# A planned attention-plus-MLP kernel: separate due times for the early work, first chunks first, and own places for minima and last sums

## The chip, the cores and the metric

The kernel runs on one core of a Trainium2 chip. The metric is the device time of one execution in microseconds (us). A core has five engines that run side by side, each in its own program order: TensorE (PE) for matmuls, VectorE (DVE), ScalarE (ACT) and GpSimd (POOL) for elementwise work, and SyncE (SP), which here issues all transfers between the main memory (HBM) and the on-chip memory (SBUF). Matmuls write into eight accumulation banks (PSUM). An engine waits only where an instruction needs something that another engine or a transfer has not finished.

## The reference

Inputs are `q`, `k`, `v` of 4 sequences x 8 heads x 768 positions x 64, and two weight matrices, `w_in` (512 x 2048) and `w_out` (2048 x 512). What is computed, cut to its core:

```python
keep = (pos_k < n_global) | ((rel >= 0) & (rel < n_local))     # 8 global keys, 96 local ones
scores = q @ k.T / sqrt(64) - slope[head] * dist               # then -1e9 where not keep
a = exp(scores - max(scores)); a = a / (sum(a) + 1e-9)
x = heads of (a @ v) side by side                              # 3072 tokens x 512
h = x @ w_in
out = (h * cos(h)) @ w_out                                     # 3072 x 512
```

## The kernel before

**Tiling.** The 3072 tokens are eight chunks of 384: two for each of the four sequences. The second chunk of a sequence needs 96 keys of the chunk ahead of it, the first does not, so of its four 96-row blocks the first has a window of 96 columns where all others have 200. For each chunk there are four pairs of heads (`plan_unit`, `plan_values`), 32 pairs in all: load keys and queries, scores on PE, a fold of the two halves of the window (L559) and a subtract-and-minimum (L568) on DVE, `exp` on ACT (L593), reciprocal (L604), normalisation (L616 where the block is the short one, else L621) on DVE or POOL, transposes on PE (L683), two masked copies (L691, L696) on DVE, the product with `v` on PE (L718), and a split of the result into a rounded high part and a rest (`xh` L735, `xl` L739). The first eight pairs ("exact") multiply in one pass (L542); later ones split keys and queries into two parts (`plan_split`) and use L546.

The MLP runs in 128 steps, each a chunk with one 128-wide block of the hidden layer (`plan_step`): 12 matmuls against `w_in` (L754, "first product"), an argument reduction (ACT L771, DVE L774), the cosine (ACT L777), a product (DVE L814), a split into `gh` and `gl` (L823, L827), and 9 matmuls against `w_out` (L765, "second product"). The sums over the blocks stay in PSUM until `plan_store` copies them out. `plan_weights` loads the 64-bit weight words (512 KB a block and matrix) and joins them into high part and rest, with work for ACT, DVE and POOL (L392 to L424).

**What sets the order.** Every operation goes into a planner (`Plan`) with the engines that may run it, a rough cost on each, the places it needs, and possibly a due time. `dues` carries due times backwards: an operation's due is the smaller of its own and what those that need it leave it. `run` then plays the program through with those costs: a free engine takes the ready operation with the earliest due, and one that several engines may run goes to the one where wait plus cost times `WEIGHT` is least. The outcome is a fixed program order for each engine. `PHASES` gives the order of steps: the first six blocks for chunk 0, then sixteen for chunk 1, then the remaining ten for chunk 0, then chunk by chunk. `DEPTH` is how far ahead of the transfers SP may run in the play.

**Fills.** `emit` puts matmuls of zeros (L1068, "fills") on PE where its plan shows a gap in the first 100 us: ten at the head, and one for every 250 ns of a gap beyond 150 ns (500 ns in the first 7 us). A fill thus marks a planned gap.

**Due times before.** `xdue` gives the four pairs of chunk 0 dues 5000 apart and those of chunk 1 6000 apart (`EARLY`); later chunks follow `MARGIN` and `EACH`. A step's due is its number times `PERIOD`; weights have no due of their own.

**The rest touched.** `worst` (L584) is one 128 x 8 tile: after a pair's minima are in its `st` tile, DVE folds them into `worst`. At the end `flag` reduces `worst` to a word (L873), every engine reads it (L1010) and branches over a general path that does not run (L1011). The output copies `oo` (L849) of all chunks use the two places `wu`, shared with the weights' scratch; the third copy of a chunk so needs the first one's store to have finished.

Of the kernel before, what the change touches and what calls it, by code (L numbers as in the profile page):

```python
# [10 lines left out]
F32 = mybir.dt.float32  # L11
# [34 lines left out]
MARGIN, EACH = 3.2, 3.2  # L46
EARLY = {0: 5000, 1: 6000}
WEIGHT = {PE: 1, ACT: 0.5, DVE: 1.2, POOL: 0.6}

PHASES = [(0, 0, 6), (1, 0, 16), (0, 6, 16)]  # L50

PIECES = {-1: [(0, 128), (128, 384)]}
NT, NST, NPV, NX, NV, NRAW, NQK, NRR, NG = 5, 5, 3, 2, 3, 3, 2, 3, 2

DEPTH = 3000

# [191 lines left out]
class Net:  # L248
# [26 lines left out]
    def constants(self):  # L275
# [47 lines left out]
        g.memset(self.half_pi, math.pi / 2)  # L323
        self.worst = self.const.tile([P, 2 * CT], F32, name="worst")
        g.memset(self.worst, -3.0e38)
# [46 lines left out]
    def plan_weights(self, f):  # L372
# [5 lines left out]
        ends = []  # L378
        for kind, src, out in (("wi", cols, self.wi), ("wo", rows, self.wo)):
            raw = self.const.tile([P, 512, 2], U32, name="raw", tag=f"{kind}{f}")  # L380
# [51 lines left out]
            o = p.op({ACT: 525, DVE: 335, POOL: 595}, whigh, [o], [wu], port=True)  # L432
            ends.append(p.op({DVE: 600, POOL: 1260}, wrest, [o], [wu], port=True))
        return ends


    def plan_loads(self, n, b2):


        nc, p, D = self.nc, self.plan, self.D  # L440
        b, c = divmod(n, self.NCH)
        W = 2 * UB * D
        t0 = c * CW
        lead = 1 if c == 0 else 0
        vs = Slot(self.early("v", n, b2), lambda i: self.work.tile([SLOT, 1 + CT, W], F32, name="v", tag=i))
        L = dict(n=n, first=c == 0, v=vs)
        src = self.v[b][:, b2 * W : (b2 + 1) * W]
        nt = 1 + CT - lead
        s = t0 - (1 - lead) * R

        def blocks(e):
            nc.sync.dma_start(vs.tile[:R, lead:], src[s : s + nt * R].rearrange("(t p) d -> p t d", p=R))

        def glob(e):
            nc.sync.dma_start(
                vs.tile[R:, lead:CT], src[:G].rearrange("p (t d) -> p t d", t=1).broadcast_to([G, CT - lead, W])
            )

        L["lv"] = [
            p.op({SP: 470}, blocks, [], [vs], extra=290 * nt),  # L460
            p.op({SP: 470}, glob, [], [vs], extra=46 * CT),
        ]
        return L
# [18 lines left out]
    def plan_unit(self, L, pr):  # L482
# [6 lines left out]
        n, first = u["n"], u["first"]  # L489
        b, c = divmod(n, self.NCH)  # L490
        u["hs"] = slice((pr % UB) * P, (pr % UB + 1) * P)
# [25 lines left out]

        st = u["st"] = Slot("st", lambda i: self.work.tile([R, 6 * CT], F32, name="st", tag=i))
        tt = u["tt"] = [
# [8 lines left out]
        for js, h in [(js, h) for js in (((0, 1),) if exact else ((0,), (1,))) for h in range(0, CT, 2)]:  # L528
# [25 lines left out]
            for j, ps in pss.items():  # L554
# [7 lines left out]
                for i, t in enumerate(ts):  # L562

                    def least(e, i=i, t=t, j=j, ps=ps):
# [10 lines left out]
                            scalar=3.0e38,  # L575
                            accum_out=st.tile[:, at : at + 1],
                        )
# [3 lines left out]
        n2 = 2 * CT  # L581

        def worst(e):
            nc.vector.tensor_tensor(self.worst[:R], self.worst[:R], st.tile[:, :n2], op=ALU.max)  # L584

        self.chain("worst", p.op({DVE: 100}, worst, [o for _, o in ttr], [st], due=self.xdue(n, pr), port=True))
        exps = []
        for (t, j), o in ttr:

            def exp(e, t=t, j=j):  # L590
                x = tt[t // 2].tile[:, t % 2, j, : width(t)]
                c = 2 * t + j
                nc.scalar.activation(  # L593
                    x, x, AF.Exp, bias=st.tile[:, c : c + 1], scale=-1.0, accum_out=st.tile[:, n2 + c : n2 + c + 1]
                )

            exps.append(p.op({ACT: 365}, exp, [o], [tt[t // 2], st], table="exp"))

        def add(e):
            x = st.tile[:, n2 : 2 * n2]  # L600
            nc.vector.tensor_scalar(x, x, 1e-9, None, op0=ALU.add)

        def rec(e):
            nc.vector.reciprocal(st.tile[:, 2 * n2 :], st.tile[:, n2 : 2 * n2])  # L604

# [3 lines left out]
        for h in range(0, CT, 2):  # L609

            def norm(e, h=h):
                x = tt[h // 2].tile.rearrange("p t j w -> p (t j) w")
                r = st.tile[:, 2 * n2 + 2 * h : 2 * n2 + 2 * h + 4].rearrange("p (c o) -> p c o", o=1)
                if lead(h):
# [129 lines left out]
    def xdue(self, n, pr):  # L744
        rest = self.NP - 1 - pr
        first = next(s for s, x in enumerate(self.seq) if x[0] == n)
        if n in EARLY:
            return first * PERIOD - rest * EARLY[n]
        return int((first - MARGIN - rest * EACH) * PERIOD)
# [29 lines left out]
    def plan_step(self, s, n, f, a, b):  # L779

        nc, p = self.nc, self.plan
        due = s * PERIOD
        x = self.x[n]
# [57 lines left out]
    def plan_store(self, n, t, po, o, keep, due):  # L841
# [5 lines left out]
        else:  # L847
            oo = Slot("wu", lambda i: self.work.tile([P, 512], F32, name="oo", tag=i))
        if before is not None and keep:  # L849
# [11 lines left out]
        if keep:  # L861
            return
        r0 = n * CW + t * P
        p.op({SP: 470}, lambda e: nc.sync.dma_start(self.out[r0 : r0 + P, :], oo.tile), [o], [oo], extra=730)


    def flag(self):
# [4 lines left out]
        fi = self.small.bitcast(I32)[0:1, 15:16]  # L872
        nc.vector.tensor_reduce(c[:, 0:1], w, axis=mybir.AxisListType.X, op=ALU.max)  # L873
        nc.vector.tensor_scalar(c[:, 0:1], c[:, 0:1], -FILL - 1024.0, None, op0=ALU.is_le)
# [262 lines left out]
```

## Time and profile before

| what | value |
|---|---|
| time, median of 3 | 696.05 us (695.97 to 697.09) |
| the profiled execution's own time | 695.79 us |
| its span, first to last instruction | 694.1 us |
| PE busy | 680.9 us (98%) |
| DVE busy | 485.3 us (70%) |
| ACT busy | 459.2 us (66%) |
| POOL busy | 172.0 us (25%) |
| fills | 55, 16.1 us of PE's busy time |

The span is what the trace covers; the time around it is 1.7 us. Busy time of PE includes the fills, which compute nothing, so PE is to be read stage by stage: in which stretch it does matmuls of the computation, and in which it fills or waits. An idle engine costs nothing unless something that sets the end waits for it.

### The profile page before, as it was taken

How to read it: one execution, taken by the hardware profiler on the slowest of the kernel's cores; microseconds unless marked ns; L12 is line 12 of the kernel's file. 1: busy time of each engine (PE TensorE's matmuls, PEld its weight loads, DVE VectorE, ACT ScalarE, POOL GpSimd, SP SyncE). 2: the span in 40 equal slices, each digit the busy share in tenths (PEclk: the TensorE clock that was granted, in tenths of full speed). 3: DMA queues.
4: the chain of work that ended last, by engine and by line, in shares of the span. 5: the costliest groups of instructions: out<-in, count | busy, mean ns of one | idle time of the engine just before them, and what ended most of it. 6: DMA issues, size and time to landing. Idle time of an engine off the chain costs nothing.

```text
span 694.1 us, 12978 instructions
## 1 busy us (share of the span) xinstructions
PE 680.9 (98%) x4473; PEld 594.3 (86%) x4473; DVE 485.3 (70%) x1477; ACT 459.2 (66%) x1144; POOL 172.0 (25%) x221
## 2 busy tenths in 40 slices
PE   7999999999999999999999999999999999999995
PEld 4667899889898988989889888888889888898994
DVE  7998888987648877577757777477773787534342
ACT  7899986889746675576646666476663766544442
POOL 5666645553202121111111112011120111200000
PEclk9999999999999999999999999999999999999999
DMA  8999601215204222032321321132230300001001
GB/s 283 304 344 285 174 1 48 59 47 139 64 1 114 64 60 60 1 106 65 69 69 38 105 65 48 44 102 60 53 95 0 115 27 1 1 1 46 0 1 51
DMA packets 32603, 55.74 MB, mean 80 GB/s; under 512 B 3472, under 2 KB 18192, under 8 KB 32528
## 3 DMA queue, kind: packets, MB, share of 16 engines
q1 hardware_dynamic: 32528, 54.82, 27.5%
q8 instruction: 37, 0.61, 0.4%
q14 instruction: 38, 0.31, 0.2%
HBM read 48.52 MB, written 6.29 MB: 79 GB/s over the span
## 4 chain that ended last, share of the span: by engine, by line
PE 84%; ACT 5%; DVE 4%; DMA 4%; POOL 1%; issue 1%; SPq 0%; ACTq 0%; POOLq 0%; DVEq 0%
PE bank L765 36%; PE bank L754 36%; PE bank L546 5%; PE bank L718 5%; PE bank L683 2%; DMA raw<-in_qk_dram 2%; DMA raw<-in_w_out_dram 1%; ACT tt L593 1%; DVE tt L568 1%; POOL tt L616 1%; ACT L593 1%; ACT L777 1%; DVE bank L559 1%; ACT rr L777 0%; ACT raw L408 0%
## 5 line engine op out<-in xcount | busy, mean ns | idle before, releaser
L754 PE MATMUL bank<-xh,w 128*128 128x384 f32 x1024 | 296.9, 342 | 0.0
L765 PE MATMUL bank<-w,gh 128*128 128x512 f32 x768 | 245.5, 401 | 0.0
L754 PEld LDWEIGHTS bank<-xh,w 128*128 128x128 f32 x1024 | 188.2, 188 | 8.3 <-DVE rr L814 0.6
L754 PE MATMUL bank<-xl,w 128*128 128x384 f32 x512 | 172.9, 338 | 0.2 <-DVE xl L739 0.2
L765 PEld LDWEIGHTS bank<-w,gh 128*128 128x128 f32 x768 | 137.8, 188 | 20.1 <-issue 0.3
L765 PE MATMUL bank<-w,gl 128*128 128x512 f32 x384 | 151.5, 394 | 0.0
L774 DVE SCALAR_TENSOR_TENSOR rr<-rr,bank 128x384 f32<-128x384 int32 x129 | 70.1, 544 | 105.1 <-ACT rr L771 104.9
L771 ACT ACTIVATE rr<-bank 128x384 int32<-128x384 f32 x129 | 62.3, 483 | 119.8 <-PE bank L754 115.8
L777 ACT ACTIVATE rr<-rr,half_pi 128x384 f32<-128x384 f32 x129 | 79.0, 614 | 38.3 <-DVE rr L774 37.4
L814 DVE TENSOR_TENSOR rr<-bank,rr 128x384 f32<-128x384 f32 (+1 forms) x121 | 66.6, 551 | 48.4 <-ACT rr L777 47.9
L754 PEld LDWEIGHTS bank<-xl,w 128*128 128x128 f32 x512 | 96.4, 188 | 4.3 <-DVE xl L739 0.4
L593 ACT ACTIVATE tt<-tt,st 96x104 f32<-96x104 f32 (+1 forms) x256 | 94.3, 370 | 4.8 <-DVE st L568 4.2
L765 PEld LDWEIGHTS bank<-w,gl 128*128 128x128 f32 x384 | 72.1, 188 | 17.3
L827 DVE TENSOR_TENSOR gl<-rr,gh 128x384 fp32r<-128x384 f32 x102 | 60.4, 592 | 13.2 <-ACT gh L268 5.7
L268 ACT CAST gh<-rr 128x384 fp32r<-128x384 f32 (+1 forms) x93 | 47.2, 509 | 31.6 <-DVE rr L814 21.8
L272 POOL TENSOR_SCALAR ks<-raw 128x408 fp32r<-128x408 f32 (+1 forms) x32 | 18.2, 569 | 192.6 <-PE bank L546 190.2
L568 DVE CUSTOM_DVE_ANT_0 tt<-bank,dd 96x104 f32<-96x104 f32 (+1 forms) x256 | 55.3, 257 | 2.6
L718 PEld LDWEIGHTS bank<-pv,v 104*64 104x64 f32 (+1 forms) x960 | 41.1, 136 | 10.9 <-issue 5.6
L546 PEld LDWEIGHTS bank<-ks,qs 128*96 128x96 f32 x384 | 46.2, 162 | 4.8
L546 PE MATMUL bank<-ks,qs 128*96 128x200 f32 (+1 forms) x384 | 48.2, 254 | 0.0
L593 ACT ACTIVATION_READ_ACCUMULATOR tt<-tt,st 96x1 f32 x256 | 48.1, 188 | 0.0
L718 PE MATMUL bank<-pv,v 104*64 104x96 f32 (+1 forms) x960 | 47.2, 248 | 0.0
(98 smaller groups left out, 749.1 us busy)
## 6 DMA issues: line engine op xcount, KB each, us to landing
raw<-in_qk_dram SPq DMA_DIRECT2D x48, 224.0 KB
raw<-in_qk_dram SPq DMA_DIRECT2D x48, 198.0 KB
raw<-in_w_in_dram SPq DMA_DIRECT2D x16, 512.0 KB
raw<-in_w_out_dram SPq DMA_DIRECT2D x16, 512.0 KB
out_dram<-oo SPq DMA_DIRECT2D x24, 256.0 KB
v<-in_v_dram SPq DMA_DIRECT2D x16, 240.0 KB
v<-in_v_dram SPq DMA_DIRECT2D x16, 192.0 KB
raw<-in_qk_dram SPq DMA_DIRECT2D x4, 448.0 KB
```

The lines of the kernel that those rows point to most:

```text
L268: self.nc.scalar.copy(out, x)
L546: nc.tensor.matmul(out, qs[:, m, q0], ks[:, k : k + w], start=m == 0, stop=m == 1)
L568: nc.vector.tensor_tensor_reduce(tt[t // 2].tile[:, t % 2, j, :w], ps.tile[:R, i * WIN : i * WIN + w], self.dd[:, v, :w], op0=ALU.add, op1 ...
L593: nc.scalar.activation(x, x, AF.Exp, bias=st.tile[:, c : c + 1], scale=-1.0, accum_out=st.tile[:, n2 + c : n2 + c + 1])
L718: nc.tensor.matmul(px.tile[j * D : (j + 1) * D, t * R : (t + 1) * R], vs.tile[:k, t + c, hs][:, j * D : (j + 1) * D], pv[:k, c, o : o + R] ...
L754: self.nc.tensor.matmul(ph[:, :CW], self.wi[f][:, w, kk * P : (kk + 1) * P], xx[:, kk, :], start=kk == 0 and m == 0, stop=kk == self.NK - ...
L765: self.nc.tensor.matmul(po, gg[:, ts], self.wo[f][:, w, :], start=start and m == 0, stop=stop and m == 2)
L771: self.nc.scalar.activation(r.bitcast(I32), ph, AF.Copy, scale=1.0 / TWO_PI, bias=0.25)
L774: self.nc.vector.scalar_tensor_tensor(r, r.bitcast(I32), -TWO_PI, ph, op0=ALU.mult, op1=ALU.add)
L777: self.nc.scalar.activation(r, r, AF.Sin, bias=self.half_pi)
L814: {DVE: dve}, lambda e, r=r, h=h, y=y: nc.vector.tensor_tensor(y(), h(), r(), op=ALU.mult), [o], [ph, rr]
L827: self.eng(e).tensor_tensor(g[1][:, cs], y(), g[0].bitcast(F32)[:, cs], op=ALU.subtract)
```

## The change

Each of the first eight pairs gets its own due (`PAIRS`), each of the 32 weight blocks too (`BLOCKS`; 200000 lies later than any need, so such a block keeps the due of its users), and 24 steps get an offset (`STEPS`). `WEIGHT` of ACT goes from 0.5 to 0.6 and of POOL from 0.6 to 0.5, `DEPTH` from 3000 to 2000. `ORDER` takes the first chunks of all four sequences ahead of the second ones, so that chunk 1 of the program is now a first chunk; `PHASES` starts with five blocks of chunk 0, not six. `worst` becomes 128 x 32 x 8: DVE's subtract-and-minimum writes straight into a pair's own eight columns, `exp` reads them there, and the running maximum is gone. The last chunk's output copies take the three places `part`.

```diff
-EARLY = {0: 5000, 1: 6000}
-WEIGHT = {PE: 1, ACT: 0.5, DVE: 1.2, POOL: 0.6}
-PHASES = [(0, 0, 6), (1, 0, 16), (0, 6, 16)]
+PAIRS = [-26500, 14500, 18000, -11000, 9200, 17700, 28200, 34200]
+BLOCKS = [
+    200, -1800, 13200, 200000, 14600, 200000, 16100, 200000, 200000, 35900, 200000, 32700, 200000, 200000,
...
+STEPS = [
+    2000, 1000, 0, 1000, 0, 0, -2000, 0, 0, 4000, 0, 0, -4000, -2000, 0, 1000, -1000, 1000, 2000, -6000,
...
+WEIGHT = {PE: 1, ACT: 0.6, DVE: 1.2, POOL: 0.5}
+ORDER = [0, 2, 4, 6, 1, 3, 5, 7]
+PHASES = [(0, 0, 5), (1, 0, 16), (0, 5, 16)]
...
-DEPTH = 3000
+DEPTH = 2000
...
-        self.worst = self.const.tile([P, 2 * CT], F32, name="worst")
+        self.worst = self.const.tile([P, self.B * self.NCH * self.NP, 2 * CT], F32, name="worst")
         g.memset(self.worst, -3.0e38)
...
-            ends.append(p.op({DVE: 600, POOL: 1260}, wrest, [o], [wu], port=True))
+            ends.append(p.op({DVE: 600, POOL: 1260}, wrest, [o], [wu], due=BLOCKS[2 * f + i], port=True))
...
-        b, c = divmod(n, self.NCH)
+        b, c = divmod(ORDER[n], self.NCH)
...
-        st = u["st"] = Slot("st", lambda i: self.work.tile([R, 6 * CT], F32, name="st", tag=i))
+        lows = self.worst[:R, n * self.NP + pr]
+        st = u["st"] = Slot("st", lambda i: self.work.tile([R, 4 * CT], F32, name="st", tag=i))
...
-                            accum_out=st.tile[:, at : at + 1],
+                            accum_out=lows[:, at : at + 1],
...
-        self.chain("worst", p.op({DVE: 100}, worst, [o for _, o in ttr], [st], due=self.xdue(n, pr), port=True))
...
-                    x, x, AF.Exp, bias=st.tile[:, c : c + 1], scale=-1.0, accum_out=st.tile[:, n2 + c : n2 + c + 1]
+                    x, x, AF.Exp, bias=lows[:, c : c + 1], scale=-1.0, accum_out=st.tile[:, c : c + 1]
...
-        if n in EARLY:
-            return first * PERIOD - rest * EARLY[n]
+        u = n * self.NP + pr
+        if u < len(PAIRS):
+            return PAIRS[u]
...
-        due = s * PERIOD
+        due = s * PERIOD + (STEPS[s] if s < len(STEPS) else 0)
...
-            oo = Slot("wu", lambda i: self.work.tile([P, 512], F32, name="oo", tag=i))
+            cls = "part" if n == self.B * self.NCH - 1 else "wu"
+            oo = Slot(cls, lambda i: self.work.tile([P, 512], F32, name="oo", tag=i))
...
-        nc.vector.tensor_reduce(c[:, 0:1], w, axis=mybir.AxisListType.X, op=ALU.max)
+        nc.vector.tensor_reduce(c[:, 0:1], w.rearrange("p a b -> p (a b)"), axis=mybir.AxisListType.X, op=ALU.max)
```

How the engines' program order moves is shown at three places. In the changed kernel L1081 is the fill, L557 the exact scores, L693 the transposes, L728 the product with `v`, L765 the first product and L776 the second.

PE ahead of the third step of L754 (L765 in the change), before:

```order
L754 MATMUL bank<-xh,w 128x384
L542 MATMUL bank<-raw 96x200 x4
L1068 LDWEIGHTS zeros
L1068 MATMUL idle<-zeros 128x512
...
L542 MATMUL bank<-raw 96x200 x4
L1068 MATMUL idle<-zeros 128x512
...
L542 MATMUL bank<-raw 96x200 x4
...
L683 MATMUL bank<-ident,tt 104x96 x4
...
L683 MATMUL bank<-ident,tt 104x96 x4
L754 MATMUL bank<-xh,w 128x384
L754 MATMUL bank<-xl,w 128x384
```

and of the change (a first chunk, so that the score rows are 96 and 200 wide):

```order
L557 MATMUL bank<-raw 96x200 x4
L728 MATMUL bank<-pv,v 64x96 x14
L1081 LDWEIGHTS zeros
L1081 MATMUL idle<-zeros 128x512
L557 MATMUL bank<-raw 96x96 x2
L557 MATMUL bank<-raw 96x200 x2
...
L557 MATMUL bank<-raw 96x200 x4
L1081 MATMUL idle<-zeros 128x512
L765 MATMUL bank<-xh,w 128x384
L765 MATMUL bank<-xl,w 128x384
L765 MATMUL bank<-xh,w 128x384 x2
L765 MATMUL bank<-xl,w 128x384
```

From the second L754 step to the third, the order of before has gaps of 5, 4, 4 and 5 fills; the change has gaps of 1, 5 and 1, and one of 6 between its first and its second L765 step. Over the whole program the rows count 55 fills before (10 at the head, 24 more ahead of the first L754, 21 after it) and 44 now (10 at the head, 21 ahead of the first L765, 13 after it, the longest run being 13 between the transposes and the product of an early pair); the last run stood after three first products and one second, now after two first products.

DVE in chunk 0, around the first early pair's rest `xl`, before (L584 is the running maximum, L621 a normalisation):

```order
L601 TENSOR_SCALAR st<-st 96x8
L584 TENSOR_TENSOR worst<-worst,st 96x8
L604 RECIPROCAL st<-st 96x8
L568 ISA tt,st<-bank,dd 96x104
L568 ISA st 96x1
...
L584 TENSOR_TENSOR worst<-worst,st 96x8
L621 TENSOR_TENSOR tt<-tt,st 96x416
L739 TENSOR_TENSOR xl<-bank,xh 128x384
L691 TENSOR_TENSOR pv<-bank,others 104x192
```

and of the change:

```order
L706 TENSOR_TENSOR pv<-bank,own 96x384
L611 TENSOR_SCALAR st<-st 96x8
L614 RECIPROCAL st<-st 96x8
L583 ISA tt,worst<-bank,dd 96x104
...
L583 ISA tt,worst<-bank,dd 96x104
L583 ISA worst 96x1
L574 COPY_PREDICATED bank<-mine,bank 96x2x96 x2
L574 COPY_PREDICATED bank<-mine,bank 96x96 x2
L583 ISA tt,worst<-bank,dd 96x96
...
L749 TENSOR_TENSOR xl<-bank,xh 128x384
```

Gone from DVE are the running maximum and the normalisations. Up to its eighth `xl`, DVE issued 8 running maxima and 9 normalisations of a half (8 of them L621), now none; folds of two windows fall from 24 to 16 and masked copies of four blocks from 24 to 16, with as many narrower ones in their stead. POOL does all of these normalisations (L626, L631). In the whole program POOL's `gl` go from 18 to 91 (full width) and its `gh` from 23 to 91; from DVE go 73 `gl`, from ACT 69 `gh`. The scores of L546 at 200 columns go from 336 to 352 and those at 96 from 48 to 32; of L542 200-wide ones go from 56 to 48.

SP at the end, before (L864 issues the stores, L1010 reads the word):

```order
L635 DMA raw<-in_qk_dram 64x896 x2
L864 DMA out_dram<-oo 128x512 x5
L1010 TENSOR_LOAD small
L1010 ISA x2
L864 DMA out_dram<-oo 128x512
L1011 COMPARE_AND_BRANCH
```

and of the change:

```order
L469 DMA v<-in_v_dram 8x4x128
L645 DMA raw<-in_qk_dram 64x896 x2
L877 DMA out_dram<-oo 128x512 x6
L1023 TENSOR_LOAD small
L1023 ISA x2
L1024 COMPARE_AND_BRANCH
```

The sixth store of the run now stands ahead of the read of the word; before, the last store stood behind it.

## Rows read from the trace of the kernel before

**Rows 1.** Windows: busy us (count) of PE, PEld, DVE, ACT, POOL; clock, DMA share, GB/s.

```profile
core 0 of [0], span 694.1 us
0.00:54.00 54.00, 49.19 (x410) 31.55 (x412) 48.23 (x222) 46.69 (x154) 34.54 (x66) 1.00 0.96 312
54.00:100.00 46.00, 45.85 (x317) 39.85 (x313) 39.55 (x91) 45.90 (x101) 27.99 (x25) 1.00 0.60 158
300.00:680.00 380.00, 379.13 (x2425) 339.05 (x2422) 243.51 (x721) 223.84 (x550) 51.76 (x68) 1.00 0.17 48
```

**Rows 2.** The fills by line: duration ns min/median/max, first and last start us.

```profile
L1068 PE MATMUL idle<-zeros x55: 376/379/634, 1.1 to 53.4; 128*128 128x512 bf16 x55
```

**Rows 3.** Timeline of TensorE: start us, length us; fills and their counts.

```profile
1.05 4.35 PE L1068 MATMUL idle<-zeros 128*128 128x512 bf16 x10 [1.05 <-DVE zeros L278]
...
37.81 1.25 PE L1068 MATMUL idle<-zeros 128*128 128x512 bf16 x5
...
39.95 1.04 PE L1068 MATMUL idle<-zeros 128*128 128x512 bf16 x4
...
41.90 1.04 PE L1068 MATMUL idle<-zeros 128*128 128x512 bf16 x4
...
43.18 1.24 PE L1068 MATMUL idle<-zeros 128*128 128x512 bf16 x5
```

**Rows 4.** Timeline of the end, all engines.

```profile
685.45 1.29 ACT L268 COPY oo<-bank 128x512 f32<-128x512 f32 x2 [2.44 <-PE bank L765]
...
686.42 0.40 PE L765 MATMUL bank<-w,gl 128*128 128x512 f32 x1
...
688.19 0.59 ACT L268 COPY oo<-bank 128x512 f32<-128x512 f32 x1 [1.45 <-DMA out_dram<-oo]
```

**Rows 5.** Stores of the last chunk, by tile: duration ns, first and last start us.

```profile
L864 SPq DMA_DIRECT2D out_dram<-oo x3: 332/332/335, 686.1 to 688.8; - x3
```

**Rows 6.** Sequencers at the end, by line: duration ns, starts.

```profile
L1010 SPq TENSOR_LOAD <-small x1: 495/495/495, 687.1 to 687.1; - x1
...
L1010 SPq FUSED_REGOPS  x1: 186/186/186, 687.7 to 687.7; - x1
```

**Rows 7.** The branch over the general path, by line.

```profile
L1011 SPq COMPARE_BRANCH  x1: 50/50/50, 689.2 to 689.2; - x1
```

**Rows 8.** Waits of SyncE in the last 11 us: total, times, longest.

```profile
SPq L1011 <- SPq L1011: 2.9, 1, 2.9
```

**Rows 9.** VectorE groups by form: busy us, mean ns.

```profile
L691 DVE TENSOR_TENSOR pv<-bank,others 104x384 f32<-104x384 f32 x48 | 26.3, 547 | 1.4 <-PE bank L683 1.4
...
L621 DVE TENSOR_TENSOR tt<-tt,st 96x416 f32<-96x416 f32 x35 | 20.7, 609 | 0.0
...
L559 DVE COPY_PREDICATED bank<-mine,bank 96x192 f32<-96x192 uint32 x96 | 33.0, 355 | 4.0 <-PE bank L546 3.4
...
L559 DVE COPY_PREDICATED bank<-mine,bank 96x96 f32<-96x96 uint32 x32 | 7.8, 255 | 2.4 <-PE bank L546 2.2
...
L691 DVE TENSOR_TENSOR pv<-bank,others 104x192 f32<-104x192 f32 x16 | 5.7, 354 | 1.5 <-ACT pv L268 1.0 <-POOL tt L621 0.2
```

**Rows 10.** The line of the running maximum: duration ns min/median/max.

```profile
L584 DVE TENSOR_TENSOR worst<-worst,st x32: 109/164/994, 15.8 to 593.8; 96x8 f32<-96x8 f32 x32
```

**Rows 11.** The tile xl, first 90 us: first and last start.

```profile
L739 DVE TENSOR_TENSOR xl<-bank,xh x8: 543/556/558, 17.5 to 76.4; 128x384 fp32r<-128x384 f32 x8
```

**Rows 12.** Chain of waits: start us, us, what.

```profile
90.26 2.12 PE bank L754 x12
```

**Rows 13.** GpSimd groups by form: busy us, mean ns.

```profile
L827 POOL TENSOR_TENSOR gl<-rr,gh 128x384 fp32r<-128x384 f32 x18 | 18.2, 1013 | 22.5 <-PE bank L683 12.7 <-ACT gh L268 9.4
...
L621 POOL TENSOR_TENSOR tt<-tt,st 96x416 f32<-96x416 f32 x13 | 11.3, 877 | 14.6 <-DVE st L604 7.6 <-PE bank L683 3.2 <-ACT qs L638 2.2
...
L616 POOL TENSOR_TENSOR tt<-tt,st 96x208 f32<-96x208 f32 x6 | 4.5, 756 | 0.0
...
L616 POOL TENSOR_TENSOR tt<-tt,st 96x192 f32<-96x192 f32 x6 | 3.0, 503 | 11.2 <-DVE st L604 8.5 <-DVE st L568 2.7
```

More of the change, by code (lines that the diff above doesn't have):

```diff
@@ L46 @@
 MARGIN, EACH = 3.2, 3.2
-EARLY = {0: 5000, 1: 6000}
-WEIGHT = {PE: 1, ACT: 0.5, DVE: 1.2, POOL: 0.6}
-PHASES = [(0, 0, 6), (1, 0, 16), (0, 6, 16)]
+PAIRS = [-26500, 14500, 18000, -11000, 9200, 17700, 28200, 34200]
+BLOCKS = [
+    200, -1800, 13200, 200000, 14600, 200000, 16100, 200000, 200000, 35900, 200000, 32700, 200000, 200000,
+    44000, 200000, 200000, 200000, 50600, 38000, 200000, 200000, 200000, 200000, 200000, 55700, 70200,
+    200000, 69900, 200000, 200000, 200000,
+]
+STEPS = [
+    2000, 1000, 0, 1000, 0, 0, -2000, 0, 0, 4000, 0, 0, -4000, -2000, 0, 1000, -1000, 1000, 2000, -6000,
+    -1000, 14000, -1000, -3000,
+]
+WEIGHT = {PE: 1, ACT: 0.6, DVE: 1.2, POOL: 0.5}
+ORDER = [0, 2, 4, 6, 1, 3, 5, 7]
+PHASES = [(0, 0, 5), (1, 0, 16), (0, 5, 16)]
 PIECES = {-1: [(0, 128), (128, 384)]}
 NT, NST, NPV, NX, NV, NRAW, NQK, NRR, NG = 5, 5, 3, 2, 3, 3, 2, 3, 2
-DEPTH = 3000
+DEPTH = 2000
 EXACT = 8
@@ L378, in plan_weights @@
         ends = []
-        for kind, src, out in (("wi", cols, self.wi), ("wo", rows, self.wo)):
+        for i, (kind, src, out) in enumerate((("wi", cols, self.wi), ("wo", rows, self.wo))):
             raw = self.const.tile([P, 512, 2], U32, name="raw", tag=f"{kind}{f}")
@@ L489, in plan_unit @@
         n, first = u["n"], u["first"]
-        b, c = divmod(n, self.NCH)
+        b, c = divmod(ORDER[n], self.NCH)
         u["hs"] = slice((pr % UB) * P, (pr % UB + 1) * P)
@@ L581, in plan_unit @@
         n2 = 2 * CT
-        def worst(e):
-            nc.vector.tensor_tensor(self.worst[:R], self.worst[:R], st.tile[:, :n2], op=ALU.max)
-        self.chain("worst", p.op({DVE: 100}, worst, [o for _, o in ttr], [st], due=self.xdue(n, pr), port=True))
         exps = []
@@ L599, in add @@
         def add(e):
-            x = st.tile[:, n2 : 2 * n2]
+            x = st.tile[:, :n2]
             nc.vector.tensor_scalar(x, x, 1e-9, None, op0=ALU.add)
         def rec(e):
-            nc.vector.reciprocal(st.tile[:, 2 * n2 :], st.tile[:, n2 : 2 * n2])
+            nc.vector.reciprocal(st.tile[:, n2:], st.tile[:, :n2])
         o = p.op({DVE: 195}, add, exps, [st], port=True)
@@ L612, in norm @@
                 x = tt[h // 2].tile.rearrange("p t j w -> p (t j) w")
-                r = st.tile[:, 2 * n2 + 2 * h : 2 * n2 + 2 * h + 4].rearrange("p (c o) -> p c o", o=1)
+                r = st.tile[:, n2 + 2 * h : n2 + 2 * h + 4].rearrange("p (c o) -> p c o", o=1)
                 if lead(h):
@@ L862, in plan_store @@
             return
-        r0 = n * CW + t * P
+        r0 = ORDER[n] * CW + t * P
         p.op({SP: 470}, lambda e: nc.sync.dma_start(self.out[r0 : r0 + P, :], oo.tile), [o], [oo], extra=730)
```

## The prediction

> **What bounds the kernel now.** I read the windows first. Between 300 and 680 us PE is busy 379.13 of 380 us at full granted clock, while DVE has 243.51, ACT 223.84 and POOL 51.76 [rows 1]: a chain of matmuls without holes, in which the others are hidden as long as they come in time. So the edits can move the end in two places: where PE does not compute yet, and behind its last matmul. The first is the first 54 us. PE shows 49.19 us busy there [rows 1], but all 55 fills run between 1.1 and 53.4 us [rows 2], so that much of this busy time computes nothing. DVE has 48.23 and ACT 46.69 of those 54 us, and the transfer engines a share of 0.96 [rows 1]: those that feed PE are close to full, and they pace it. From 54 to 100 us PE is dense and ACT has 45.90 of 46 us: it just keeps up.
>
> PE's timeline shows what a hole costs. Ten fills at the head run from 1.05 us while the first keys come in; nothing in the change moves them. Between 37 and 45 us fills run for 1.25, 1.04, 1.04 and 1.24 us [rows 3]. These groups hold 18 fills in 4.57 us, 0.254 us a fill; a fifth fill in a group adds 0.21 us (1.25 - 1.04).
>
> At the other end the last matmul starts at 686.42 and takes 0.40 us, but the third output copy starts only at 688.19, released by the store of the first [rows 4]. SP has read the word in the meantime (at 687.1, 0.495 us) [rows 6], issues the third store at 688.8 [rows 5] and branches at 689.2 [rows 7]; 2.9 us later it goes on [rows 8], and what follows is closing down.
>
> **The change part by part.** The sum goes against the profiled execution's own time, 695.79 us; its span is 694.1 [rows 1], and the median of the runs shown lies 0.26 us above it.
>
> Fewer gaps in the first 54 us. The order has 45 fills behind the head before and 34 in the change: 11 x 0.254 = 2.8 us less. With the price of one further fill (0.21) it is 2.3. The far end is what DVE is relieved of up to the eighth early `xl`: 8 normalisations x 0.609 = 4.9, 8 narrower folds x (0.355 - 0.255) = 0.8, 8 narrower masked copies x (0.547 - 0.354) = 1.5 [rows 9], 8 running maxima x 0.164, their median, = 1.3 [rows 10]; together 8.5 us. All of it would count only if DVE alone paced PE, but ACT has as many `exp` as before and was as full. The near end is no gain at all, if the relief meets another limit. I take 2.8, since it stands nearest to holes that the trace shows, and keep 0 and 8.5 as ends. That the gaps can close is plausible: the eighth `xl` starts at 76.4 us [rows 11], the second chunk now starts after five steps and so needs it one step earlier, and the twelve matmuls of a first product take 2.12 us [rows 12], those of a step with the second product about twice that, 4.2 us, against 8.5 us of relief.
>
> The last copies. With three places the third copy waits for its matmuls alone: 686.42 + 0.40 = 686.82, and a hand-over of 0.03 as at the first copy. It then ends 0.59 later, near 687.45, not 688.78 [rows 4]: 1.3 us. But SP's read of the word no longer lies beside that wait; it stands behind the third store in SP's order. From 687.48 the issue of 0.33 [rows 5], the read of 0.495 and the register work of 0.19 [rows 6] with some 0.25 of steps between them bring the branch to about 688.75 instead of 689.2: 0.45 us less. Ends: 0, if PE's own branch is then last, and 1.3.
>
> The maximum over 256 columns at the end in place of 8 stands on DVE, beside the last matmuls (the final one starts at 686.42 [rows 4]); it costs nothing, and if that cover were gone, a few tenths of a microsecond by the masked copies' 0.547 for 384 columns [rows 9]. The larger fill of `worst` at the start, on POOL, lies beside the first load that ACT waits for: nothing, else as little.
>
> More columns. Sixteen of the two-part scores grow by 104 columns, eight exact ones shrink by as many. By the first product (2.12 us for 12 x 384 columns [rows 12]) 104 columns are 0.048 us: 16 x 0.048 - 8 x 0.048 = 0.4 us more on a full PE; ends 0 (other work of PE in the same place waits less) and 0.8.
>
> Work moved to POOL later on. 73 `gl` go there from DVE and 69 `gh` from ACT or DVE. A `gl` takes 1.013 us on POOL [rows 13]. I cost it at nothing: in both orders other matmuls of at least 9 us, at 2.12 us per twelve [rows 12], stand between a step's first and second product, and POOL, with 51.76 of 380 us busy [rows 1], gets 74 us of `gl` (73 x 1.013) over the whole run and no more than as much again of `gh`, a quarter of the time. If that cover failed in each step by only 0.1 us, 120 steps would cost 12 us.
>
> Here the traces already show a caution. DVE's running maximum, which reads two tiles in SBUF, takes 0.109 us at best and 0.994 at worst [rows 10], about the length of a `gl` on POOL [rows 13]. The Trainium skill (SBUF — State Buffer, Who interferes with whom) says that a DVE instruction with two SBUF inputs and a GpSimd instruction that reads SBUF exclude each other, and that whichever starts second "fully blocks". The row agrees with that rule for the worst case. By the rule the change, which about doubles POOL's work, has more such meetings and the sum moves towards the second rival's 700.2 below; by the row's median of 0.164 they are rare, and the sum stays.
>
> Sum: 695.79 - 2.8 - 0.45 + 0.4 = 692.9 us for a profiled execution; with the 0.26 us to the median 693.2. I forecast 693.2.
>
> **The rivals.** First: the gain is given back. ACT is full from 54 to 100 us [rows 1], with weights' work that the change doesn't take away. If PE arrives there 2.8 us ahead, it waits for ACT and new holes stand between 54 and 100 us, where the order has no fills. For it: 45.90 of 46 us. Against it: POOL, with 27.99 of 46, is now favoured by the weights of the planner, and running steps early is only worth what the weights' blocks allow. Then 695.79 - 0.45 + 0.4 + 0.26 = 696.0, no change.
>
> Second, on the slow side: normalisation on POOL sets the pace of the first eight pairs. A first chunk's pair takes 0.877 + 0.756 + 0.503 = 2.14 us there, one after the other [rows 13]; before, its long half could run on DVE beside the short one on POOL, so that a pair took 0.756 + 0.503 = 1.26. If each of the eight pairs comes 0.88 us later, that is 7.0 us, since PE's transposes and all behind them wait: 693.2 + 7.0 = 700.2. It decides from 0.35 us a pair on, where it eats the 2.8. For it: POOL has 34.54 of the first 54 us already [rows 1], DVE stalls against it as seen. Against: DVE's time goes to the next pair's minima, and the pairs overlap.
>
> Third: the later `gl` on POOL leave holes in the dense stretch; some 120 steps at 0.05 us give 6 us and 699. Against it stand the 9 us of slack.
>
> **How the numbers follow.** The forecast has 0.64, with its own range 690 to 694.6. The first rival has 0.19, the second 0.13, the third 0.04. About 0.2% (1.4 us) is what a measurement of this kernel can tell from no change. Faster by that means under 694.7: the forecast and 0.02 of the first rival's cases, 0.66. Slower means over 697.4: the second and third less a hundredth, 0.16. The rest is 0.18. For the range I cut off the far end of the first term at about half of its 8.5 us with the full 1.3 us of the tail (696.05 - 4.9 - 1.3 = 689.8) and above the point where the slow rivals begin: 689.5 to 697.2, which leaves about 0.16 above it and 0.04 below.
>
> **What would show it.** Right: fills end near 40 us and PE's windows from there on are full; the eighth `xl` starts some 8 us before 76.4; POOL shows all normalisations, DVE none; the third output copy follows the second without a wait for a store, and SP branches about 1.8 us behind PE's last matmul. Wrong: idle time of PE behind GpSimd's normalisations or behind ACT's weight work; fills that last until 50 us and more; waits of PE for `gl` after 100 us; or a median above 694.7 with all these in place, in which case the fills were never the measure of the lost time.

## The result: 690.09 us, and the profile after

The changed kernel takes 690.09 us (median of 4 runs, 689.86 to 690.58), the kernel before 696.03 in the same comparison; the ratio is 0.9914, 95% interval 0.9902 to 0.9925. I had forecast 693.2: the time moved by 5.94 us and not by 2.85. The windows of the profile after, in the columns of [rows 1]:

```profile
0.00:54.00 54.00, 48.06 (x441) 32.63 (x441) 47.52 (x236) 48.02 (x171) 38.10 (x75) 1.00 0.93 319
54.00:100.00 46.00, 45.51 (x279) 40.50 (x275) 38.61 (x70) 44.28 (x88) 27.91 (x26) 1.00 0.53 141
300.00:680.00 380.00, 379.59 (x2444) 339.65 (x2443) 199.26 (x613) 197.10 (x491) 174.11 (x212) 1.00 0.17 48
```

PE looks as full as before, and POOL has more than three times its work from 300 to 680 us. Yet PE gets through 2444 matmuls there and not 2425. The fills by line, against [rows 2]:

```profile
L1081 PE MATMUL idle<-zeros x44: 377/379/631, 1.1 to 43.2; 128*128 128x512 bf16 x44
```

And the tile xl in the first 90 us, against [rows 11]:

```profile
L749 DVE TENSOR_TENSOR xl<-bank,xh x8: 549/558/560, 17.4 to 67.3; 128x384 fp32r<-128x384 f32 x8
```

The last fill starts 10 us earlier, the eighth xl 9. GpSimd's groups by form, against [rows 13]:

```profile
L838 POOL TENSOR_TENSOR gl<-rr,gh 128x384 fp32r<-128x384 f32 x91 | 92.5, 1016 | 7.6 <-PE bank L693 1.5
...
L631 POOL TENSOR_TENSOR tt<-tt,st 96x416 f32<-96x416 f32 x48 | 42.3, 885 | 34.5 <-DVE qs L652 20.7 <-DVE gl L838 12.1 <-DVE st L614 1.7
...
L626 POOL TENSOR_TENSOR tt<-tt,st 96x208 f32<-96x208 f32 x16 | 10.1, 631 | 0.0
...
L626 POOL TENSOR_TENSOR tt<-tt,st 96x192 f32<-96x192 f32 x16 | 8.1, 506 | 24.0 <-DVE w L437 5.6 <-DVE qs L652 4.8 <-DVE worst L583 4.4
```

All normalisations run there now (48 + 16 + 16), at 885, 631 and 506 ns (877, 756 and 503 before). All waits of PE that the trace names from 100 to 680 us are one row (total us, times, longest):

```profile
PE bank L693 <- POOL tt L631: 0.2, 1, 0.2
```

The end: its timeline, against [rows 4].

```profile
679.79 1.98 ACT L281 COPY oo<-bank 128x512 f32<-128x512 f32 x3 [2.38 <-PE bank L776]
...
680.75 0.39 PE L776 MATMUL bank<-w,gl 128*128 128x512 f32 x1
```

SP's branch over the general path by line, against [rows 7], and SP's wait behind it, against [rows 8]:

```profile
L1024 SPq COMPARE_BRANCH  x1: 50/50/50, 683.1 to 683.1; - x1
```

```profile
SPq L1024 <- SPq L1024: 3.1, 1, 3.1
```

The three copies are one piece without a wait for a store. SP branches 1.9 us behind the last matmul (2.4 before), but what follows takes 3.1 us (2.9 before).

**A ledger.** Busy shares can't say where 5.9 us went, since PE is near 100% in both. So I add up the starts of the matmuls. Each trace holds the same 4,416 of the computation. Each kind gets one fixed time, near its usual pitch (the time from one start to the next): 174.5 ns in the first product, 233.5 in the second, 90 or 44 for scores by their columns, 90 for a transpose, 46.5 for a product with `v`; together 647.8 us in every kernel. What the starts take beyond that is "lost" time of PE, fills included. By stretches, in us, with the number of the experiment:

```
kernel                                    0:54  54:100  100:250  250:end   all
before                                   25.00    1.82     3.42     8.79  39.03
after                                    22.93    1.24     3.83     5.36  33.36
before, new weights from 100 us on (1)   25.28    1.86     4.76     9.89  41.79
after, old weights from 100 us on (2)    22.79    1.15    10.56     6.04  40.54
after, old weights from 250 us on (13)   22.74    1.31     3.57     6.00  33.62
before, all shifted by 992 bytes (3)     25.09    1.77     3.49     8.87  39.22
after, old output copies (4)             22.73    1.09     3.58     5.36  32.76
before, banks of after (5)               25.03    1.90     3.47     8.87  39.27
after, banks of before (6)               22.87    1.39     3.86     5.34  33.46
before, least scores by block (7)        22.07    5.89     3.55     6.58  38.09
after, without own dues (8)              23.43    6.17     5.09     5.87  40.56
before, places of after (9)              25.21    1.92     2.97     7.04  37.14
after, places of before (10)             23.07    1.67     4.14     6.98  35.86
before, small tile of 128 bytes (11)     25.48    1.60     2.80     7.09  36.97
after, small tile of 96 bytes (12)       22.59    1.44     4.60     6.92  35.55
after, gh and gl 32 bytes off (14)       23.29    1.42     4.02     6.41  35.14
after, gh and gl 64 bytes off (15)       23.70    1.29     3.66     3.56  32.21
```

How far the ledger scatters is seen in kernels alike but for the last copies, an equal shift or the banks: after and experiments 4 and 6 differ by up to 0.3 us in a stretch before 250 us and by 0.02 behind it; before and experiments 3 and 5 by 0.1. Between before and after, 2.65 us were gained up to 100 us (26.82 to 24.17), close to the 2.8 forecast there, and 3.0 behind it (12.21 to 9.19), all of it from 250 us on (from 100 to 250 us after loses 0.4 more), where I had forecast nothing. From the last matmul to the end it is 0.24 more (7.25 to 7.01). The experiments are about the 3.0.

### The profile page after: what moved, and what is told of

Read it like the earlier page. It is cut to its first block, busy times and chain, and to the rows that moved or that the text cites. A ratio compares the mean times of both kernels' runs of the same rounds, so it can differ in the third digit from the quotient of the medians.

```text
span 688.2 us, 12961 instructions
## 1 busy us (share of the span) xinstructions
PE 674.0 (98%) x4462; PEld 591.2 (86%) x4462; DVE 417.9 (61%) x1313; ACT 416.3 (60%) x1064; POOL 332.7 (48%) x427
## 4 chain that ended last, share of the span: by engine, by line
PE 85%; ACT 6%; POOL 3%; DMA 2%; issue 2%; DVE 2%; SPq 0%; POOLq 0%; ACTq 0%
PE bank L776 37%; PE bank L765 36%; PE bank L728 5%; PE bank L561 5%; PE bank L693 2%; ACT tt L603 2%; DMA raw<-in_w_out_dram 1%; POOL ks L661 1%; POOL tt L631 1%; DMA out_dram<-oo 1%; DMA raw<-in_qk_dram 1%; POOL gl L838 1%; ACT L788 1%; DVE tt L583 0%; ACT w L281 0%
## 5 line engine op out<-in xcount | busy, mean ns | idle before, releaser
L765 PE MATMUL bank<-xh,w 128*128 128x384 f32 x1024 | 299.3, 342 | 1.0 <-DVE gl L838 0.8
L776 PE MATMUL bank<-w,gh 128*128 128x512 f32 x768 | 244.2, 399 | 0.0
L765 PEld LDWEIGHTS bank<-xh,w 128*128 128x128 f32 x1024 | 188.2, 188 | 9.5 <-DVE gl L838 1.8
L765 PE MATMUL bank<-xl,w 128*128 128x384 f32 x512 | 172.3, 336 | 0.0
L776 PEld LDWEIGHTS bank<-w,gh 128*128 128x128 f32 x768 | 137.9, 188 | 19.6 <-ACT tt L603 0.3
L776 PE MATMUL bank<-w,gl 128*128 128x512 f32 x384 | 151.4, 394 | 0.0
L285 POOL TENSOR_SCALAR gh<-rr 128x384 fp32r<-128x384 f32 x91 | 46.8, 514 | 210.4 <-PE bank L776 151.4
L765 PEld LDWEIGHTS bank<-xl,w 128*128 128x128 f32 x512 | 96.4, 188 | 4.0
L603 ACT ACTIVATE tt<-tt,worst 96x104 f32<-96x104 f32 (+1 forms) x256 | 94.4, 370 | 6.6 <-DVE worst L583 5.7
L838 POOL TENSOR_TENSOR gl<-rr,gh 128x384 fp32r<-128x384 f32 (+1 forms) x93 | 93.6, 1007 | 8.5 <-PE bank L693 1.5
L776 PEld LDWEIGHTS bank<-w,gl 128*128 128x128 f32 x384 | 72.3, 188 | 16.7
L631 POOL TENSOR_TENSOR tt<-tt,st 96x416 f32<-96x416 f32 x48 | 42.3, 885 | 34.5 <-DVE qs L652 20.7
L661 POOL TENSOR_TENSOR ks<-raw,ks 64x512 fp32r<-64x512 f32 (+1 forms) x39 | 47.9, 1227 | 5.4 <-POOL gl L838 2.5
L728 PEld LDWEIGHTS bank<-pv,v 104*64 104x64 f32 (+1 forms) x960 | 41.0, 136 | 9.2 <-issue 7.0
L603 ACT ACTIVATION_READ_ACCUMULATOR tt<-tt,worst 96x1 f32 x256 | 48.0, 188 | 0.0
```

The source lines that it names most:

```text
L603: nc.scalar.activation(x, x, AF.Exp, bias=lows[:, c : c + 1], scale=-1.0, accum_out=st.tile[:, c : c + 1])
L661: self.eng(e).tensor_tensor(ks[D:, k0:], raw.tile[D:, k0:KW], ks.bitcast(F32)[D:, k0:], op=ALU.subtract)
L728: nc.tensor.matmul(px.tile[j * D : (j + 1) * D, t * R : (t + 1) * R], vs.tile[:k, t + c, hs][:, j * D : (j + 1) * D], pv[:k, c, o : o + R] ...
L765: self.nc.tensor.matmul(ph[:, :CW], self.wi[f][:, w, kk * P : (kk + 1) * P], xx[:, kk, :], start=kk == 0 and m == 0, stop=kk == self.NK - ...
L776: self.nc.tensor.matmul(po, gg[:, ts], self.wo[f][:, w, :], start=start and m == 0, stop=stop and m == 2)
L838: self.eng(e).tensor_tensor(g[1][:, cs], y(), g[0].bitcast(F32)[:, cs], op=ALU.subtract)
```

## The experiments

Times are medians; the ratio is to the kernel before on the same chip. The kernel after stands at 0.9914 (0.9902 to 0.9925). The theories weighed: of the split, the late gain comes from work that moved to POOL; of the places, from where the tiles lie in SBUF; of the banks, from which PSUM bank a sum lies in.

**1. The new weights alone, late, in the kernel before.**

```diff
-cost = lambda x: wait(x) + o.engines[x] * WEIGHT[x]
+cost = lambda x: wait(x) + o.engines[x] * (WEIGHT if t < 100000 else LATER)[x]
```

> The kernel before, but from 100 us of the plan's clock on each free operation chooses its engine by the new weights (ACT 0.6, POOL 0.5); the early plan, the addresses and the chunks' order are those of before. The comparison of the two traces left 2.8 us that were gained between 100 us and the last matmul. If they come from the lighter VectorE and ScalarE (theory of the split): about 693.2 us, 2.8 under before, with the second product's median pitch near 231.5 ns and not 233.4. If they come from where the tiles lie in SBUF (theory of the places) or from the order of the chunks: 696.0, pitch 233.4. If POOL's longer copies make holes, as the third rival had it: 697 to 699.

699.43 us, ratio 1.0043 (1.0029 to 1.0057): slower. All of PE's named waits from 100 to 680 us:

```profile
PE bank L766 <- ACT oo L269: 1.3, 2, 0.7
PE bank L755 <- DVE rr L815: 0.9, 1, 0.9
```

The named waits are 2.2 us; the ledger loses 2.4 us more than before behind 100 us. In the profiled run 0.6 us of the loss lie outside the traced span (2.3 us there, 1.7 before), and no view shows why. The time is the third rival's, but these rows name ACT and DVE, not a `gl` on POOL. In the order of before, the new weights cost and do not gain.

**2. The old weights, late, in the kernel after.** The same edit the other way round.

> The kernel after, but from 100 us of the plan's clock on with the weights of before (ACT 0.5, POOL 0.6), so that 48 normalisations, some 70 copies gh and some 70 gl go back to VectorE and ScalarE. Theory of the split: 2.8 us of the gain are lost, about 692.9 us, pitch of the second product back near 233.4 ns. Theory of the places, or of the order of the chunks: 690.1, pitch 231.5.

697.52 us, 1.0019 (1.0010 to 1.0028). It looks like the theory of the split, and isn't: the loss is one event. A wait of PE from 150 to 200 us, and the windows (columns as in [rows 1]):

```profile
PE bank L694 <- DVE tt L627: 2.7, 1, 2.7
```

```profile
150.00:160.00 10.00, 6.14 (x50) 5.40 (x50) 9.29 (x45) 9.65 (x33) 3.70 (x5) 0.96 0.32 93
160.00:170.00 10.00, 10.00 (x60) 9.33 (x57) 4.86 (x10) 3.92 (x8) 2.23 (x2) 0.70 0.38 104
```

PE is busy 6.14 of 10 us, behind a normalisation on DVE, and after that the granted clock is 0.70 of full over the next 10 us: part of them at the lower of its two levels, 1.2 instead of 2.4 GHz. In 100 to 250 us it loses 10.56 and not 3.83 us; from 250 us on 6.04, far nearer to the 5.36 of after than to 8.79. The weights so are not what made most of the late stretch's gain.

**3. All addresses shifted alike.**

```diff
+pad = self.const.tile([P, 248], F32, name="pad")
```

> The kernel before with one unused tile of 992 bytes a partition behind the tile worst: every constant and weight lies 992 bytes higher, where it lies in the kernel after (32 bytes off a multiple of 64, before on one); the order on every engine is that of before, but for one memset at the start. Theory of the places: 693.2 us (2.8 under before), pitch 231.5 ns. Theory of the split or of the order: 696.0, pitch 233.4.

696.03 us, 1.0000 (0.9991 to 1.0009). An equal shift of all tiles does nothing. My expectation was too coarse: it called this "where the tiles lie", but the padding left their distances as they were.

**4. The old output copies in the kernel after** (class `wu` instead of `part`).

> The kernel after, with the last block's three output copies in the class of two buffers again, so that the third copy waits for the first store. My step: SP's last branch comes 0.45 us later behind the last matmul (2.4 and not 1.97 us); the run 0.2 to 0.45 us slower, 690.3 to 690.5. Rival (what follows the branch takes it back, as 0.2 of the 0.45 seemed to be): 0 to 0.25.

690.16 us, 0.9917 (0.9903 to 0.9930). In its trace the third copy waits for a store again, SP branches 2.4 us behind the last matmul and not 1.9, and the span ends 7.30 us behind it and not 7.01: my mechanism. But 0.07 us between the medians is within what the runs scatter. The rival's range holds it and mine misses it, though the scatter can't exclude the low end of mine.

**5 and 6. The PSUM banks swapped.** Unused tiles ahead of the program fix which bank each name gets.

```diff
+for i in "05673124":
+    self.psum.tile([P, 512], F32, name="first", tag=f"b{i}")
```

> The kernel before, order and SBUF addresses untouched; only which PSUM bank each buffer name gets is that of the kernel after: the second product's three sums lie in banks 6, 4, 7 and not 5, 6, 7, the first product's two in 0 and 5 and not 4 and 0. In the runs so far the second product's pitch in the last stretch followed the kernel it was derived from (before: 229 to 238 ns by position, after: 233 at every place), not the weights, not the addresses. Theory of the banks: the pitch pattern turns into that of after, and the run gains what the pitch is worth, some 900 matmuls by 1.8 ns, 1.6 us: 694.4 us. Theory of the instruction stream (its alignment or its waits) or of the chunks' order: pattern as before, 696.0.

> The kernel after with the banks of before (second product 5, 6, 7, first product 0 and 4). Theory of the banks: pattern of before in the last stretch (229 to 238 ns by position), 1.6 us lost, 691.7 us. Theory of the instruction stream or of the order: 233 ns at every place, 690.1.

696.15 us, 1.0000 (0.9991 to 1.0009), and 690.08 us, 0.9918 (0.9904 to 0.9931). Neither time nor pattern moved. The theory of the banks fell.

**7. The least scores by block, alone, in the kernel before** (`worst` 128 x 32 x 8, `st` 64 bytes and not 96, no running maximum; all else as before).

> The kernel before with one part of the change: the least scores are kept by block, the running maximum (64 operations on VectorE) is gone. The plan then sets 46 fills and not 55. By my early step each fill behind the head costs 0.254 us: 9 of them, 2.3 us, 693.7 us; the split of the late work, POOL's share above all, stays that of before. Rival (the running maximum hid beside other work, the fills only mark waits that stay): 696.0.

694.59 us, 0.9978 (0.9969 to 0.9987). The ledger shows more than the median: 2.93 us gained up to 54 us, 4.07 given back from 54 to 100, and 2.21 gained from 250 us on. The first rival's hand-back, in two windows:

```profile
60.00:65.00 5.00, 3.46 (x39) 3.31 (x38) 4.42 (x19) 4.97 (x20) 2.74 (x3) 0.82 1.05 296
65.00:70.00 5.00, 5.00 (x35) 4.23 (x36) 4.19 (x10) 4.04 (x8) 2.75 (x2) 0.84 1.04 377
```

PE runs short while ACT is full (4.97 of 5 us), and the clock falls. But ACT was as full there before (4.96, with PE at 5.00), and the longest wait that the trace names is for a `gl` on DVE (1.5 us): that ACT is the cause is not shown. Most of the late gain (2.21 of 3.43 us) is in this kernel, without the new weights and without the new order of chunks. The running maximum is 32 operations in the trace, not the 64 of my expectation.

**8. The kernel after without its tables of dues.**

> The kernel after without the three tables of dues (early pairs, weights' blocks, steps); the two constants of before stand in their place. The plan sets 51 fills and not 44, and gives the PSUM buffers the banks of before. By my early step: 7 fills by 0.254 us, 1.8 us slower, 691.9; if the banks count as well (1.6 us), 693.5. Rival (the dues are not what saves the fills' time): 690.1.

697.47 us, 1.0020 (1.0011 to 1.0029): 7.4 us lost where I expected 1.8. 4.93 of them lie from 54 to 100 us, where again PE runs short and the clock falls:

```profile
54.00:60.00 6.00, 4.31 (x36) 3.95 (x37) 5.08 (x18) 5.47 (x14) 5.46 (x7) 0.61 1.05 249
60.00:65.00 5.00, 5.00 (x24) 4.63 (x24) 2.00 (x5) 3.78 (x9) 2.52 (x4) 0.79 1.03 275
```

Up to 54 us, seven more fills cost only 0.50. The dues do not save fills so much as keep this stall away; the three tables went together, so which of them does it is open. The count of fills, 51, told nothing of it.

**9 and 10. The places swapped.** Unused tiles at the start fix the order in which the working tiles are laid into SBUF; the program's order is untouched.

```diff
+for i, w in (("tt0", 416), ("tt1", 416), ...):
+    self.work.tile([P, w], F32, name="first", tag=i)
```

> The kernel before, its order untouched, with the working tiles laid into SBUF in the order of the kernel after: xh, rr, gh, gl, ks, qs and the rest then lie to each other and to the weights exactly as there (the two pairs gh 3,072 bytes apart and not 18,432), all of it 992 bytes lower. The equal shift alone did nothing (the padded kernel), the banks did nothing; but every kernel with the smaller tile st showed the pitch of after. Theory of the relative places: the pattern of after in the last stretch (second product 233 ns at every position), and the losses of 250 to 650 us fall from 8.7 to about 6.5 us, as where only the least scores were kept by block: 2.1 us or a little more, 693.7 us. Rival (the running maximum itself, 64 operations on VectorE, slowed the products): pattern as before, 696.1.

> The kernel after with its working tiles laid as in the kernel before (shifted by the 992 bytes that did nothing). Theory of the relative places: the pattern of before (229 to 238 ns by position) and 2.1 us lost, 692.2 us. Rival: 233 ns at every position, 690.1.

693.55 us, 0.9962 (0.9949 to 0.9976), and 692.76 us, 0.9960 (0.9947 to 0.9974): 2.4 gained, 2.7 lost. The chain of waits from 640 to 654 us shows what changes on PE (start, us, what; a piece is all matmuls of one product). Before, after, before with the places of after, and after with those of before:

```profile
640.77 2.09 PE bank L765 x9
642.86 2.09 PE bank L754 x12
```

```profile
641.46 2.08 PE bank L765 x12
643.53 2.10 PE bank L776 x9
```

```profile
641.06 2.08 PE bank L754 x12
643.14 2.10 PE bank L765 x9
```

```profile
641.78 2.09 PE bank L776 x9
643.87 2.09 PE bank L765 x12
```

The durations go with the places, not with the program: 2.09 and 2.09, or 2.08 and 2.10. Matmul by matmul, the second product takes 229, 230, 230, 232, 238, 237, 231, 234, 231 ns with the places of before and 232, then seven times 233, then 231 with those of after, whichever kernel it is. In this last stretch the sums are nearly equal; most of the gain from 250 us on (1.36 of 1.75 us in before) lies ahead of it, from 250 to 600 us, where the attention's matmuls run between the products. Yet it is the products that gain. Behind 100 us, their starts within a product lose 8.3 us in before and 5.8 with the places of after; 6.8 in after and 9.0 with those of before. The attention's matmuls stay: 1.9 and 2.0 us, and 1.3 and 1.2 under their fixed times.

The places are not all of the 3.0 us. Behind 100 us the ledger gives them 2.20 us in before and 1.93 in after. The rest goes with the program: from before to after the attention's matmuls gain 3.1 us, and the starts that follow a product's last matmul lose 1.6.

**11 and 12. One tile's size.** In before, each of the five `st` tiles is 96 bytes a partition, which puts xh, xl, rr, gh and gl 32 or 96 bytes beyond a multiple of 128 from the weights. In after, `st` has 64 bytes, and they lie 64 beyond one.

```diff
-st = ... self.work.tile([R, 6 * CT], F32, name="st", tag=i)     # before: 96 bytes
+st = ... self.work.tile([R, 8 * CT], F32, name="st", tag=i)     # 128 bytes
```

> The kernel before with one number changed: the small tile st is 128 bytes a partition and not 96 (five slots, the added 32 bytes unused). In the order in which before lays its tiles, everything behind an st slot then lies a multiple of 128 bytes from the weights; before it, xh, xl, rr, gh and gl lay 32 or 96 bytes off such a multiple. The two pairs gh stay far apart, as before. Theory of the 64 bytes (the pitch depends on whether products' operands lie a multiple of 64 bytes apart): the whole gain of the swapped places, 2.4 us, 693.5 us, the losses of 250 to 650 us near 6.3. Theory of the distances (how far gh, rr and xh lie from each other in whole): pattern as before, 695.9.

> The kernel after with st at 96 bytes again (16 words used, 8 unused), in its own order of places: xh, xl, rr, gh and gl come to lie 32 or 96 bytes off a multiple of 128 from the weights. Theory of the 64 bytes: 2.7 us lost as with all the places of before, 692.8 us, losses of 250 to 650 us near 7.0 and not 5.3. Theory of the distances: 690.1.

693.69 us, 0.9964 (0.9951 to 0.9978), and 693.02 us, 0.9955 (0.9941 to 0.9969). One number in the tile's shape gains 2.3 us in one kernel and loses 2.9 in the other (behind 100 us, 2.32 and 2.33 by the ledger). Whether the places are at 64 or at 0 beyond a multiple of 128 thus makes little difference to the whole. With everything at multiples of 128 the two products take other times again:

```profile
645.14 2.10 PE bank L754 x12
647.25 2.08 PE bank L765 x9
```

**13. The old weights from 250 us on, in the kernel after.**

> The kernel after, with the weights of before from 250 us of the plan's clock on, behind the stretch in which the earlier such kernel stalled; places, banks and the early plan stay those of after. In that earlier kernel the losses of 250 to 650 us were 6.0 and not 5.3 us. If the new weights carry only a small rest of the later gain: 690.5 to 690.9 us. If they carry the part of it that the places leave over and more: 691.5 or later. If they carry nothing: 690.1.

690.39 us, 0.9923 (0.9910 to 0.9937). By the ledger 0.64 us lost from 250 us on, where after and its two like kernels agree to 0.02; in the medians 0.3, which the intervals do not tell from none. If the weights carry anything there, it is a small rest.

**14 and 15. Only the second product's operands moved.** A 32-byte or a 64-byte gap ahead of `gh` and `gl` in the kernel after; the third `rr` and the output copies move with it.

> The kernel after with the four buffers gh and gl, stationary operands of the second product, 32 bytes higher, and so no multiple of 64 bytes from the weights; xh and xl, moving operands of the first product, stay at a multiple of 64. If each product's own operands decide: the second product's nine pitches in the last stretch turn to those of before (229 to 238), the first product's twelve stay those of after (175, 174, 169, 170, 176, then 173), and most of the 2.7 us goes: 691.5 to 692.8. If other tiles decide (the attention's, or xh and xl alone): 690.1.

> The kernel after with gh and gl 64 bytes higher, at a multiple of 128 bytes from the weights, and xh and xl as they are. In the kernel with the 128-byte small tile, where all lay at multiples of 128, the second product's nine matmuls took 2081 ns in the last stretch (2095 in after) and the first product's twelve 2106 (2078). If each product's own operands decide, this kernel takes the better of both: 14 ns in each of 128 steps, 1.8 us, 688.3 us. If not: 690.1, or later by what the first product loses (28 ns a step, 3.6 us).

692.75 us, 0.9949 (0.9935 to 0.9962), and 688.25 us, 0.9883 (0.9868 to 0.9898): the second is faster than both kernels, its interval clear of after's, at the time expected, but by luck. Its second product takes 2.05 us in the chain of 640 to 654 us, with the first at its 2.08:

```profile
640.81 2.08 PE bank L765 x12
642.89 2.05 PE bank L776 x9
```

By their starts the nine take 2053 ns there, 43 less than in after and not 14; from 250 to 600 us their mean pitch is 234.8 ns against 236.8, some 19 ns for nine. The 1.8 us are what these and the rest of the run leave, not 14 ns in every step.

The 32-byte gap lost more in the medians (2.7 us) than in its trace (1.8, of which 1.05 from 250 us on). Its time is in the range that I gave, its patterns are not as I expected: the second product took 2.10 as in after, at 235, 229, 236, 234, 231, 235, 233, 234 and 231 ns, which is not that of before, and the first product's moved too (177, 175, 174, 169, 170, 176). So `gh` and `gl` carry a good part, and how much of the rest belongs to `xh`, `xl` or the attention's tiles is open.

## Why the prediction was wrong

**The range: held by luck.** 690.09 lies inside 689.5 to 697.2, but I had made the low end of 4.9 us of early gain and 1.3 at the tail; the runs gave 2.65 and 0.24.

**Early gaps: right in size.** I had 2.8 for 11 fills; the ledger gives 2.65 up to 100 us, 2.07 of them in the 54 us where the fills lie. The price of a fill is no rule: up to 54 us nine fewer gained 2.93 us in experiment 7, seven more cost 0.50 in experiment 8. Both lose 4 to 5 us in a stall from 54 to 100 us with the clock falling. In experiment 7 the gain is given back as the first rival had it, though not shown to be ACT's doing; in the change the dues of its own keep the stall away.

**More columns: wrong by 0.4.** Sixteen scores grow, but 16 exact ones shrink, not eight: the trace has 112 of 200 columns before and 96 after, not the 56 and 48 that I had counted. The term is nil.

**Last copies: mechanism right, size not.** The copy waits for no store and the branch comes 0.45 us earlier, but 0.24 is left at the end of the span, and the runs of experiment 4 can't tell it from nothing.

**Work moved to POOL, costed at nothing: nearly right.** No `gl` makes PE wait behind 100 us. The second rival did not come: POOL has all normalisations at 885, 631 and 506 ns and the eighth `xl` is 9 us earlier. The meetings that I feared with DVE did come. A `gl` on POOL takes no longer (1016 ns with 91 of them, 1013 with 18), but DVE's `qs`, which reads two tiles in SBUF, does; before and after:

```profile
L642 DVE SCALAR_TENSOR_TENSOR qs<-raw,qs 128x384 fp32r<-128x384 f32 x48 | 29.3, 611 | 0.1
```

```profile
L652 DVE SCALAR_TENSOR_TENSOR qs<-raw,qs 128x384 fp32r<-128x384 f32 x48 | 33.8, 714 | 0.4 <-ACT qs L648 0.2
```

Of the 48, 16 took over 700 ns (7 before), each beside an instruction on POOL that started ahead of it, and 15 of them ended 0.41 to 0.42 us behind that one's end. They cost nothing here: no named wait of PE behind 100 us is for them. Nor were the meetings rare before, as I took them to be from a median: 8 of the 32 running maxima took over 400 ns.

**The step that failed** is the first paragraph: "So the edits can move the end in two places: where PE does not compute yet, and behind its last matmul." I took a dense PE for a PE at its limit, and so the stretch from 100 us to the last matmul had no gain in the sum. The runs showed 3.0 us there. By the ledger 1.9 to 2.3 of them came out of products whose matmuls run closer to each other, because `st` shrank from 96 to 64 bytes and the tiles behind it moved. The diff shows both sizes (`6 * CT`, `4 * CT`), and I read it only as work taken from DVE. Shown by swapping places alone (2.4 and 2.7 us in the medians) and the one size alone (2.3 and 2.9).

By the ledger alone, 2.65 up to 100 us, 0.24 at the end and 1.9 to 2.3 by the places make 4.8 to 5.2 of 5.9 us. The weights late (experiment 13, one trace) may hold 0.4 to 0.6 more. What is left, up to 0.7, is open: no experiment has the order of chunks alone, or the running maximum alone.

## What to carry to other kernels

A row that shows PE 99% busy says that it never waits, not that it can't go faster: add up its starts by kind before calling a stretch fixed. When an edit changes a tile's size, even a small scratch tile, look at where it moves the operands of the matmuls, and try a pad. A saved gap is only saved if the stretch behind it keeps up: here stalls of 1.5 to 4 us cost 4 to 7 with the clock.

## What the runs showed of the hardware

- Where SBUF tiles lie relative to each other changes the pitch of these matmuls, by up to 4% of a single one (229 to 238 ns in one product) and 0.3 to 0.4% of this kernel's time. An equal shift of all and other PSUM banks did nothing. The pattern in the last stretch is the same whether POOL works there or not (experiments 1 and 3), so it is not POOL's writes (busy 18.21 and 0.00 of the 50 us from 620 to 670). The Trainium skill (TensorE: Matmul & The Clock Gate, Step-by-step: what each phase is for) says that PE reads the streaming and the stationary operand through two independent ports, so that loading weights takes no read bandwidth from the running matmul. These runs can't test that by itself. The same nine matmuls took 2.05 or 2.10 us by where `gh` and `gl`, their stationary operands, lay; whether the two reads collide, or something else does, no run here shows.
- Between 1.5 and 4 us of a starved PE went with a granted clock of 0.61 to 0.84 in the window of it or just behind it (experiments 2, 7, 8).
- DVE's `qs`, which reads two tiles in SBUF, takes 0.56 us in the median and up to 1.10 where an instruction on POOL started ahead of it; in the kernel after it then ended 0.41 to 0.42 us behind that one in 15 of 16 cases.
